# A rewritten order table for an attention and mixing kernel: GpSimd work set apart from VectorE work with two SBUF inputs

## The chip, the core and the metric

The kernel runs on one core of a Trainium2 chip. A core has five instruction queues that run side by side and wait for each other by semaphores: TensorE (PE, with its weight loads shown as PEld), VectorE (DVE), ScalarE (ACT), GpSimd (POOL) and SyncE (SP), which here issues every DMA. The metric is the device time of one execution in microseconds.

## The reference

Four batches of 768 tokens with 8 heads of 64 go through a windowed attention and then a mixing block.

```python
k_sum = k.reshape(B, H, nb, 32, D).max(axis=3)          # 24 block maxima
v_sum = v.reshape(B, H, nb, 32, D).mean(axis=3)         # 24 block means
scores_l = scale * q @ k.T     # only |i - j| < 16 is kept
scores_s = scale * q @ k_sum.T + log(32)
a = exp(scores - max); a = a / (sum(a) + 1e-9)
x = a @ concat(v, v_sum)                                # then [B, 768, 512]
theta = x @ w_theta
y = w_tok_r @ (x * cos(theta)) + w_tok_i @ (x * sin(theta))
u = x + y
out = u + max(u @ w_ch, 0)
```

The four weight matrices come as 64-bit floats and are turned into 32-bit floats on the core.

## The kernel before

The program is first written down as a list of 2525 operations with their dependences (`Program.op`), and then issued in the order of a table, `ORDER` (`Program.issue`). A row of the table such as `V+743,-707` names an engine (P, A, V, G, S for PE, ACT, DVE, POOL, SP) and the numbers of operations, each as a step from the number before. So the table sets two things: in which order each engine meets its instructions, and on which engine an operation runs where several may run it. Buffers of the pools `r` (52 of 512 words), `w` (17 of 1024), `l` (19 of 384) and the 8 PSUM banks `b` are handed out in the order of the table. No engine is told to wait for another but by data and by buffers.

```python
def hi_op(dst, src, n, reads, writes, psum=False):
    op(f"AV {'psum' if psum else 'cast'} {n}", lambda e: copy(e, dst(), src()), reads, writes)
def lo_op(dst, src, hi, n, reads, writes):
    op(f"VG tt {n}", lambda e: V[e].tensor_tensor(dst(), src(), hi().bitcast(F32), op=ALU.subtract), reads, writes)
...
    for row in order.split():
        e, seqs = names[row[0]], row[1:].split(",")
...
    o.fn(e)
```

The letters at the start of an operation's kind are the engines that may run it: "AV cast" runs on ACT or DVE, "VG tt" (two tensors in SBUF) on DVE or POOL, "GAV part" and "GAV join" on any of the three.

The work, by the lines of the profile:

- Weights: each of 32 slices is loaded and turned from 64-bit to 32-bit by a magnitude (L2288 on ACT, L2290 on DVE), a clamp (L2292, DVE or POOL), a shift (L2293, DVE) and two joins of bits with two inputs (L2295, L2297, DVE). Later slices are split into a rounded high part (L2244, "AV cast") and the rest (L2250, "VG tt") for matmuls at full rate.
- Attention, 24 tiles of 128 tokens (six a batch): scores (L2390, PE), a masked minimum from PSUM (L2416, DVE), exponentials (L2420, ACT), a turn of the probabilities (on PE for the first six tiles; later by a copy into 16-bit halves, a transposing DMA and a copy back, L2244 "part" and "join"), the product with v (L2432, PE), division by the sum (L2436 to L2445). For batches 1 to 3 the keys are gathered into `k` (L2244, POOL or ACT).
- Mixing: theta (L2489, L2485, PE), its reduction, sine and cosine (L2495 to L2510, ACT, DVE or POOL), two products with x (L2517, DVE or POOL), their split (L2244, L2250), and the mixing matmuls: L2534 for batch 0, L2554 for batches 1 to 3. The result is added to u (L2568, DVE).
- Channels: w_ch is combined for Strassen's seven products (L2592, DVE or POOL), then for each batch u is combined (L2617, DVE or POOL), split (L2244 to ACT or DVE, L2250 to DVE or POOL, into the pool `l`), multiplied (L2628, PE), kept (L2244 from PSUM) and finished (L2642, L2644, DVE).

Of the kernel before, what the change touches and what calls it, by code (L numbers as in the profile page):

```python
# [19 lines left out]
B, H, S, D = 4, 8, 768, 64  # L20
# [35 lines left out]
S-646,-16,-6,-44,+48,+53,-41,-14,+8  # L56
V-3
S+1,+13,+42,-51,-55
V+48
A+53  # L60
S-44
V+45
S+28,-69
V-17
S-43
V+102,-57
P-14,+1,+1,+1,+1,+1,+1
V+66
S+8
P-73,+32  # L70
V+34
S+177
V-175
P-55
V+56
S-40,+50
P-64
V+20,+13
A-9
V+11,-16  # L80
S+259
V-257,+11
P-30
A+21
V-5
A+21
V+16
A-30
P-39
A+50  # L90
P-32
A+33
S+33
V+7
A-55
V+34
P-50
S+223
V-151
S+154  # L100
V-153
P-53
V+8
P-26
A+19
S+297
V-265
A-21
V+42
A-71  # L110
G+51
P-20
S+54
P+141
A-220
V-3
A+29
S+329
V-140
G+3  # L120
V-176
P-29
V+222,+1,-15
P-194
S+374
A-161
V-194
A-32
V+224,-223
A+13  # L130
S+589
P-351
A-250
V+13,+21,+187,-207
A+209
V-15
A+18
V-20
P-23
S-132  # L140
A+174
V+40,-58
A+5
P-256
G+79
V+1
A+148
P+43
S+370
V-560  # L150
P-80
A+254
P-25
A+42
V-197
S+218
A-209
P+147
V-155
A+178  # L160
S-81
G-88
A+168
V-171
A+231
P-81
V+576,-513,+1,+14
S-18
P-35
A+43  # L170
V-3,+1
A+1
P-66
V+79
A-54
S-157
V-7,+217
P-38
S+837
A-876  # L180
V-148
S+553
P-380
A+57
V-81
A+67
V-215
P+253
A-66,+40,+1
V-40,-39  # L190
A+40
V-180
P+221
A-80
V+23,+1
P+171
V-170
A+39
V+341
A-324  # L200
V-210,+1
P+277
V-45,+15,+2
G-261
V+245,-254
S+541
A-391
V+106
P-41,-26
A+27  # L210
S+35
P-20
V-80
G+1
V-130
A+168
P+27
V+50,-12
A-23
S+307,-289  # L220
V+19
P+126
A-177
S-145,+223
V-63,+428,-442,+15
P-42
V-182
S+551
V-3,-259
A-39  # L230
S+37
V-283
P+179
A+78
G+300
V-351
A+52,-15
G+341
V-283
P-80  # L240
A+39
P-80
V+108
G-287
S+22
V+505
A-223,-233,+150
V-149
P+108
A+78  # L250
S+272
A-287
V+43
A-42
P+16
V+25
A-104
V-185
S+536
P-309  # L260
A+68
V+7
G-116
A+107
V+236
G+164
S-679
A+280
P-44
A+42,-27,-14  # L270
S+281
A-226
V-119
S+351
V-350
A+1
G+370,-1
P-330,+159
V-82
G+252  # L280
P-328
V+312
P-275
V-265
P+251
V+51
A-36
P+29
S+35,-275
V+134,+1  # L290
P+39
V+23,+1
S+290
V-289
P+135
A-83
S+307
V-280
A-25
V-41,+67  # L300
A-104,-168
P+322
V-116
A+28
V-270
G+205
V+116
# [2454 lines left out]
```

## Time and profile before

| | us |
|---|---|
| median of 3 runs (range) | 509.34 (506.67 to 513.09) |
| the profiled execution | 505.22 |
| its span, first to last instruction | 503.4 |
| PE busy | 449.0 |
| DVE busy | 418.7 |
| ACT busy | 261.3 |
| POOL busy | 233.9 |

Busy is the time in which at least one instruction of the engine ran; about 2 us of the profiled execution lie outside the span. An instruction's duration in the profile runs from its start to its end, and it may start while the one before it on the engine still ends, so durations add up to some more than the busy time. In what follows the span is cut into five stretches, at the last mixing matmul of each batch: 0 to 184.5 us (batch 0), 184.5 to 281 (batch 1), 281 to 367.8 (batch 2), 367.8 to 432 (batch 3) and the rest, 432 to 503.4, which is channel work alone.

### The profile page before, as it was taken

What the parts mean: (1) busy time and instruction counts of PE and PEld (TensorE: products, weight loads), DVE (VectorE), ACT (ScalarE), POOL (GpSimd) and SP (SyncE); (2) the same over time, 40 slices, a digit from 0 to 9 for tenths busy, and PEclk for the clock granted to TensorE, in tenths of its full rate; (3) what the DMA queues carried; (4) which work ended last, traced back from release to release, by engine and by line L of the source; (5) the groups of instructions that cost most, each with busy time, mean ns of one, the idle gap of its engine ahead of it and who ended that gap; (6) DMA issues with size and microseconds to landing.
All of it is one profiled execution on the core that took longest, in us unless ns stands there. A gap on an engine that the chain in (4) does not pass through costs nothing.

```text
span 503.4 us, 10037 instructions
## 1 busy us (share of the span) xinstructions
PE 449.0 (89%) x3520; PEld 347.7 (69%) x3520; DVE 418.7 (83%) x1063; ACT 261.3 (52%) x572; POOL 233.9 (46%) x262
## 2 busy tenths in 40 slices
PE   8898988898979598898999799989999959977886
PEld 6474544444656466776887688878888848977875
DVE  3889999998997979987789888775558683899997
ACT  1498995866645546674866475814423301423230
POOL 0113476353675766453352644351432572645661
PEclk9999999999998889998999989999999988999899
DMA  8999978798976649537577656669463402431045
GB/s 293 348 306 280 311 210 211 190 223 247 177 218 140 179 107 204 137 103 225 143 199 167 171 114 145 143 156 250 144 203 114 175 12 80 157 125 64 16 167 210
DMA packets 108578, 88.88 MB, mean 177 GB/s; under 512 B 61936, under 2 KB 88304, under 8 KB 108528
## 3 DMA queue, kind: packets, MB, share of 16 engines
q1 hardware_dynamic: 108528, 88.24, 63.7%
q8 instruction: 28, 0.46, 0.4%
q14 instruction: 22, 0.18, 0.1%
HBM read 55.19 MB, written 18.87 MB: 147 GB/s over the span
## 4 chain that ended last, share of the span: by engine, by line
PE 21%; DVE 21%; issue 6%; POOL 6%; DMA 5%; ACT 3%; SPq 1%; DVEq 0%; POOLq 0%; ACTq 0%
PE b L2554 11%; PE b L2628 7%; DVE r L2244 4%; POOL r L2250 3%; DVE l L2250 3%; DVE r L2250 2%; DMA r<-r 2%; PE b L2485 2%; DVE r L2416 2%; ACT r L2420 2%; DVE r L2644 1%; POOL r L2244 1%; DMA u_scratch<-r 1%; POOL r L2517 1%; DMA w<-wch 1%
## 5 line engine op out<-in xcount | busy, mean ns | idle before, releaser
L2554 PE MATMUL b<-w,r 128*128 128x512 f32 x432 | 158.6, 406 | 11.0 <-DVE r L2250 7.5
L2554 PE MATMUL b<-r,r 128*128 128x256 f32 x432 | 122.6, 284 | 0.5 <-DVE st L2416 0.4
L2554 PEld LDWEIGHTS b<-w,r 128*128 128x128 f32 x432 | 82.5, 191 | 34.1 <-DVE r L2250 8.5
L2420 ACT ACTIVATE r<-r,st 128x118 f32<-128x118 f32 x192 | 63.9, 387 | 44.8 <-DVE st L2416 44.3
L2554 PEld LDWEIGHTS b<-r,r 128*128 128x128 f32 x432 | 83.1, 192 | 2.2 <-DVE st L2416 0.7
L2244 POOL COPY r<-r 128x1024 uint16<-128x1024 uint16 (+2 forms) x43 | 53.3, 1249 | 51.6 <-ACT r L2420 20.7
L2485 PE MATMUL b<-w,r 128*128 128x512 f32 x216 | 56.7, 400 | 1.0 <-DVE r L2250 0.9
L2534 PE MATMUL b<-w,r 128*128 128x512 f32 x96 | 47.3, 623 | 4.4 <-DVE w L2297 3.9
L2416 DVE CUSTOM_DVE_ANT_0 r<-b,cs 128x118 f32<-128x118 f32 x192 | 45.2, 271 | 5.8 <-PE b L2390 4.9
L2485 PEld LDWEIGHTS b<-w,r 128*128 128x128 f32 x216 | 38.5, 188 | 10.5 <-DVE r L2250 1.3
L2244 DVE COPY r<-r 118x1024 uint16<-118x1024 uint16 (+2 forms) x40 | 36.6, 923 | 8.3 <-ACT r L2420 4.2
L2250 POOL TENSOR_TENSOR l<-r,l 128x384 fp32r<-128x384 f32 x26 | 31.1, 1205 | 21.1 <-PE b L2628 13.3
L2628 PE MATMUL b<-l,r 128*128 128x384 f32 x192 | 37.9, 342 | 3.3 <-DVE r L2642 2.4
L2628 PEld LDWEIGHTS b<-l,r 128*128 128x128 f32 x192 | 34.1, 191 | 4.8 <-DVE r L2642 3.5
L2292 POOL TENSOR_SCALAR r<-r 128x512 f32<-128x512 f32 (+1 forms) x21 | 14.6, 701 | 48.4 <-DVE r L2290 30.5
L2628 PE MATMUL b<-l,w 128*128 128x384 f32 x144 | 30.6, 346 | 6.0 <-DVE r L2244 4.0
L2432 PEld LDWEIGHTS b<-v,r 118*64 118x64 f32 x768 | 25.5, 140 | 14.3 <-issue 5.1
L2244 POOL COPY k<-kn 128x188 f32<-128x188 f32 x47 | 22.9, 503 | 26.9 <-PE b L2390 24.0
L2244 ACT CAST l<-r 128x384 fp32r<-128x384 f32 x38 | 18.4, 513 | 32.5 <-PE b L2628 23.0
L2244 ACT COPY r<-r 128x944 uint16<-128x944 uint16 (+2 forms) x25 | 29.1, 1168 | 11.2 <-DMA r<-r 5.7
L2534 PEld LDWEIGHTS b<-w,r 128*128 128x128 f32 x96 | 17.8, 195 | 24.2 <-issue 16.0
L2432 PE MATMUL b<-v,r 118*64 118x65 f32 x768 | 29.1, 228 | 5.3 <-POOL r L2244 1.5
(98 smaller groups left out, 900.0 us busy)
## 6 DMA issues: line engine op xcount, KB each, us to landing
u_scratch<-r SPq DMA_DIRECT2D x40, 256.0 KB, 3.4
v<-vg SPq DMA_DIRECT2D x48, 195.0 KB, 3.4
r<-qg SPq DMA_DIRECT2D x24, 256.0 KB, 4.9
r<-u_scratch SPq DMA_DIRECT2D x32, 192.0 KB, 3.1
out<-r SPq DMA_DIRECT2D x32, 192.0 KB, 2.0
kn<-kT SPq DMA_DIRECT2D x6, 798.0 KB, 6.9
r<-u_scratch SPq DMA_DIRECT2D x16, 256.0 KB, 3.3
w<-wti SPq DMA_DIRECT2D x6, 512.0 KB, 6.6
```

The source lines that it names most:

```text
L2244: (nc.scalar.copy if e == "ACT" else V[e].tensor_copy)(dst, src)
L2250: op(f"VG tt {n}", lambda e: V[e].tensor_tensor(dst(), src(), hi().bitcast(F32), op=ALU.subtract), reads, writes)
L2292: op(f"VG ts {n}", lambda e: V[e].tensor_scalar(f(), f(), MOST, LEAST, ALU.min, ALU.max), [], [f_ref])
L2416: op("V ttr", lambda eng, n=n: nc.vector.tensor_tensor_reduce(e.get()[:, n], sc[n % 2].get()[:, 2 * a + n // 2], mask(m), -SCALE, 3.0e38, ...
L2420: op("A exp", lambda eng, n=n: nc.scalar.activation(e.get()[:, n], e.get()[:, n], AF.Exp, bias=st.get()[:, n:n + 1], scale=-1.0), [(st, n) ...
L2432: mm("av", [lambda n=n, g=g: nc.tensor.matmul(xa.get()[ROW[g], n], t.get()[:, n, ROW[g]], v[g].get()[:NK, NH * a + n], start=True, stop=Tr ...
L2485: calls = [lambda t=t, xx=xx, k=k, c=c, wt=wt: nc.tensor.matmul(th.get(), xx.get()[:, c], wt.get()[:, k], start=(c == 0 and t == 0), stop= ...
L2517: op(f"VG tt {DM}", lambda e, z=z, hc=hc: V[e].tensor_tensor(z(), xn[b, i].get().rearrange("p h d -> p (h d)")[:, None, hc].broadcast_to(( ...
L2534: nc.tensor.matmul(acc, zb[b, c // 2, s].get()[:, r, c % 2 * P:(c % 2 + 1) * P], wt[r, th].get()[:, 0], start=(clear and s == r == 0), sto ...
L2554: nc.tensor.matmul((ma[c].get(), half(2, c)())[th], z[k].get()[:, r, c * P:(c + 1) * P], wt[r, th].get()[:, kw], start=(s == r == t == 0 a ...
L2628: calls = [lambda t=t, p=p, x=x, k=k: nc.tensor.matmul(acc.get(), a(p, k, m), x.get(), start=(first and k == 0 and t == 0), stop=(k == 1 a ...
L2644: op(f"V {'ttp' if extra is None else 'tt'} {HT}", lambda e: nc.vector.scalar_tensor_tensor(y.get(), x.get(), 0.0, y.get(), ALU.max, ALU.a ...
```

## The change

Only the table `ORDER` is new; the 2525 operations, their dependences, the pools and their sizes are the same. The lines of the file move up by 75 (L2250 becomes L2175, L2244 L2169, L2617 L2542, L2420 L2345).

```diff
 ORDER = """
-G+3
-P+1,+1,+1,+1,+1,+1,+1,+1,+1,+1,+1,+1,+1,+1,+1,+1,+1,+1,+1,+1,+1,+1,+1,+1,+1,+1,+1,+1,+1
-V+743,-707,+3,+215,+3,+663,-59,-181
+V+71,-3,+221,+486
+S-715,-8,+67
+V+1,+1,+1,+1,+1
...
```

413 operations change their engine. POOL gives up 150 and takes 93, so it runs 201 instead of 258. DVE runs 898 instead of 871, ACT 509 instead of 479, PE 563 and SP 354 as before. By kind:

| operation | POOL | DVE | ACT |
|---|---|---|---|
| two inputs, 384 wide (L2250, L2617) | 45 to 18 | 43 to 70 | |
| two inputs, 512 wide (L2250, L2517) | 41 to 33 | 83 to 91 | |
| two inputs, 256 wide (L2250, L2592) | 12 to 11 | 10 to 11 | |
| turn, part and join (L2244) | 43 to 26 | 40 to 45 | 25 to 37 |
| keys into k (L2244) | 47 to 36 | | 25 to 36 |
| v's block means (L2244) | 7 to 4 | 6 to 2 | 3 to 10 |
| magnitude of the weights, 512 wide (L2288, L2290) | | 14 to 5 | 6 to 15 |

Two places of the new order. The first is the end of POOL's queue, in the channel work: `l<-r,l` is the rest of a split (L2250, now L2175), `r<-r,r` a combination of u (L2617, now L2542). Before, its last twelve instructions:

```order
L2617 TENSOR_TENSOR r_5460<-r_5001,r_5201 128x384
L2250 TENSOR_TENSOR l_5485<-r_5355,l_5470 128x384
L2250 TENSOR_TENSOR l_5501<-r_4786,l_5283 128x384
L2250 TENSOR_TENSOR l_5511<-r_5235,l_5435 128x384
L2250 TENSOR_TENSOR l_5567<-r_5001,l_5543 128x384
L2250 TENSOR_TENSOR l_5586<-r_5410,l_5572 128x384
L2250 TENSOR_TENSOR l_5597<-r_4563,l_5521 128x384
L2250 TENSOR_TENSOR l_5616<-r_5400,l_5529 128x384
L2617 TENSOR_TENSOR r_5628<-r_5218,r_5368 128x384
L2250 TENSOR_TENSOR l_5647<-r_5285,l_5642 128x384
L2250 TENSOR_TENSOR l_5672<-r_5449,l_5670 128x384
L2250 TENSOR_TENSOR l_5674<-r_5628,l_5638 128x384
```

And now:

```order
L2175 TENSOR_TENSOR l_5150<-r_4801,l_5100 128x384
L2175 TENSOR_TENSOR l_5286<-r_4930,l_5121 128x384
L2542 TENSOR_TENSOR r_5323<-r_5143,r_5053 128x384
L2175 TENSOR_TENSOR l_5364<-r_5053,l_5102 128x384
L2175 TENSOR_TENSOR l_5433<-r_4518,l_5407 128x384
L2175 TENSOR_TENSOR l_5458<-r_5244,l_5362 128x384
L2175 TENSOR_TENSOR l_5536<-r_4982,l_5534 128x384
L2175 TENSOR_TENSOR l_5569<-r_5262,l_5564 128x384
L2175 TENSOR_TENSOR l_5604<-r_5405,l_5594 128x384
L2175 TENSOR_TENSOR l_5664<-r_5517,l_5581 128x384
L2542 TENSOR_TENSOR r_5666<-r_4611,r_5221 128x384
L2175 TENSOR_TENSOR l_5670<-r_5666,l_5668 128x384
```

The kinds are the same, but the numbers at the names, which count up through the program, are spread wider: the twelve results reached from l_5485 to l_5674 before, and now from l_5150 to l_5670. What lies between went to DVE. Behind the last mixing matmul of batch 3, POOL had 32 instructions of these two kinds and now has 13.

The second place is ACT's queue around the exponentials of attention tile 9, in the first stretch. `r<-r,st` of L2420 (now L2345) are exponentials, four a half tile; `128x8x118` is a part, `118x2x512` a join. Before:

```order
L2420 ACTIVATE r_1375<-r_1375,st 128x118
L2420 ACTIVATE r_1387<-r_1387,st 128x118 x2
L2420 ACTIVATE r_1282<-r_1282,st 128x118 x2
L2420 ACTIVATE r_1375<-r_1375,st 128x118
L2420 ACTIVATE r_1387<-r_1387,st 128x118
L2495 ACTIVATE w<-b_1246 128x512
L2420 ACTIVATE r_1375<-r_1375,st 128x118 x2
L2244 COPY r_1019<-r_1375 128x8x118
L2420 ACTIVATE r_1387<-r_1387,st 128x118
```

And now:

```order
L2169 COPY r_1430<-r_1423 128x8x118
L2345 ACTIVATE r_1412<-r_1412,st 128x118 x2
L2169 COPY r_588<-r_1412 128x8x118
L2420 ACTIVATE w<-b_1277 128x512
L2169 COPY r_1535<-r_1432 128x1024
L2169 COPY r_1540<-r_1514 118x2x512
L2169 COPY r_1566<-r_1533 118x2x512
L2345 ACTIVATE r_1517<-r_1517,st 128x118 x4
L2169 COPY r_843<-r_1517 128x8x118
```

Tile 9's two joins and one of its two parts, which DVE and POOL ran before, now stand in ACT's queue, the joins ahead of the next tile's exponentials (`r_1517`); the L2420 of these rows is the line of the theta step, L2495 before.

## Rows read from the trace of the kernel before

**Rows 1.** The page: busy time by engine, and the chain that ended last

```profile
PE 449.0 (89%) x3520; PEld 347.7 (69%) x3520; DVE 418.7 (83%) x1063; ACT 261.3 (52%) x572; POOL 233.9 (46%) x262
...
PE 21%; DVE 21%; issue 6%; POOL 6%; DMA 5%; ACT 3%; SPq 1%; DVEq 0%; POOLq 0%; ACTq 0%
```

**Rows 2.** Busy by stretch: PE, PEld, DVE, ACT, POOL, clock, DMA share, GB/s

```profile
0.00:184.50 184.50, 161.69 (x1532) 100.87 (x1532) 161.81 (x512) 119.28 (x286) 85.14 (x117) 0.96 0.84 232
184.50:281.00 96.50, 89.33 (x690) 73.14 (x690) 84.47 (x209) 61.49 (x119) 47.15 (x54) 0.98 0.68 169
281.00:367.80 86.80, 82.43 (x681) 68.99 (x680) 63.34 (x171) 43.72 (x93) 35.69 (x37) 0.98 0.64 160
367.80:432.00 64.20, 58.16 (x318) 50.50 (x317) 41.74 (x66) 16.29 (x31) 27.83 (x25) 0.95 0.37 120
432.00:503.40 71.40, 57.41 (x309) 54.23 (x308) 67.28 (x109) 20.48 (x44) 38.10 (x32) 0.98 0.33 116
```

**Rows 3.** Timeline of 474 to 480 us: start, us, what, count

```profile
474.38 1.36 DVE L2250 TENSOR_TENSOR l<-r,l 128x384 fp32r<-128x384 f32 x1
...
475.28 3.90 POOL L2250 TENSOR_TENSOR l<-r,l 128x384 fp32r<-128x384 f32 x3
...
475.66 1.37 DVE L2644 SCALAR_TENSOR_TENSOR r<-r,r 128x384 f32<-128x384 f32 x1
...
476.96 0.55 DVE L2642 TENSOR_TENSOR r<-b,r 128x384 f32<-128x384 f32 x1
```

**Rows 4.** DVE instructions of single lines: duration ns min/median/max, first and last start us

```profile
L2416 DVE CUSTOM_DVE_ANT_0 r<-b,cs x192: 230/270/289, 15.9 to 330.4; 128x118 f32<-128x118 f32 x192
...
L2644 DVE SCALAR_TENSOR_TENSOR r<-r,r x24: 544/560/1369, 423.7 to 497.5; 128x384 f32<-128x384 f32 x24
L2644 DVE SCALAR_TENSOR_TENSOR r<-b,r x8: 543/548/552, 444.9 to 499.4; 128x384 f32<-128x384 f32 x8
...
L2250 DVE TENSOR_TENSOR l<-r,l x30: 543/548/1377, 370.6 to 485.1; 128x384 fp32r<-128x384 f32 x30
L2250 DVE TENSOR_TENSOR r<-w,r x13: 671/686/792, 190.2 to 413.1; 128x512 fp32r<-128x512 f32 x13
...
L2244 DVE COPY r<-r x40: 635/752/1814, 73.7 to 351.4; 118x1024 uint16<-118x1024 uint16 x17, 128x1024 uint16<-128x1024 uint16 x12, 128x944 uint16<-128x944 uint16 x11
...
L2244 DVE CAST r<-r x30: 278/419/1620, 124.0 to 427.1; 128x512 fp32r<-128x512 f32 x22, 128x256 fp32r<-128x256 f32 x8
```

**Rows 5.** Groups by line and shape: count, busy us, mean ns, idle before

```profile
L2250 POOL TENSOR_TENSOR l<-r,l 128x384 fp32r<-128x384 f32 x26 | 31.1, 1205 | 21.1 <-PE b L2628 13.3 <-ACT l L2244 5.1 <-DVE l L2244 2.6
L2250 DVE TENSOR_TENSOR r<-r,r 128x512 fp32r<-128x512 f32 x28 | 29.9, 1074 | 0.4
...
L2250 DVE TENSOR_TENSOR l<-r,l 128x384 fp32r<-128x384 f32 x30 | 23.8, 809 | 0.2 <-PE b L2628 0.2
...
L2644 DVE SCALAR_TENSOR_TENSOR r<-r,r 128x384 f32<-128x384 f32 x24 | 19.2, 820 | 0.4
...
L2244 DVE COPY r<-r 118x1024 uint16<-118x1024 uint16 x17 | 18.3, 1088 | 3.0 <-DMA r<-r 2.0 <-POOL r L2292 1.1
...
L2244 DVE CAST r<-r 128x512 fp32r<-128x512 f32 x22 | 16.6, 755 | 2.5 <-POOL r L2517 1.2 <-POOL r L2244 1.0
...
L2244 ACT COPY r<-r 118x1024 uint16<-118x1024 uint16 x7 | 9.5, 1355 | 6.0 <-DMA r<-r 4.4 <-DVE r L2250 1.6
```

**Rows 6.** The chain in order of time: start us, us, a run of channel matmuls

```profile
488.27 10.28 PE b L2628 x57
```

**Rows 7.** Who waited for whom: us in total, times, longest us

```profile
ACT r L2420 <- DVE st L2416: 44.3, 25, 5.9
...
POOL l L2250 <- PE b L2628: 13.3, 6, 4.2
...
PEld b L2534 <- DVE r L2297: 7.5, 3, 5.8
```

More of the change, by code (lines that the diff above doesn't have):

```diff
@@ new lines @@
+P-71
+V+181,-102
+G+172
+S-61
+P-155
+G+37
+S+270
+V-262
+S+8
+P+165
+V-202,-12
+S+73
+A-57
+V-2,-3
+A+7
+V-5,-16
+A+7
+P-42
+V+36
+A+19
+V+212
+P-266
+S+248
+A-196
+V-16
+P-35
+V+266
+A-228
+P-37
+V+267
+A-229
+P+16
+S+36
+A-54
+V+215
+P-250
+V+249,-189
+A-6
+P-15
+V+212,-175
+S+166
+P-187
+G+189
+A-204
+V+28
+A+187
+S+174
+P-388
+V+28
+A+184,+1
+G-193
+P+233
+S+89
+V-327
+A+212
+V-3,-13
+A+17
+V-227,+1
+S+52
+V-38
+A-13
+V+14
+P+282
+V-278
+A+194
+V-193
+A+204
+S+368
+A-551
+V-20
+P+163
+A+43
@@ new lines @@
+G-185
+P+172
+V+53
+A-82
+V+81
+P-38
+V+41
+S-20
+V+5
+A-189
+V-38
+P+160
+A+71
+S-8
+V-184,+1,+1
+A+202
+P-82
+V+80,-15,-1
+A+19,-42,-14
+P-26
+S-17
+A-125
+P+143
+A-47
+V-74
+S+533
+V-559
+S+547
+P-360
+A-39
+V+64,-121
+P+82
+G-72
+A+128
+V-41
+A+28
+V-27
+G-40
+V+41
+P+156
+A-133,+1
+G-209
+S+247
+A-22
+V+27
+S+306
+V-413
+A+24
+G+426,+181
+V-775
+P+225
+A-80
+V+24
+S-160
+V+161
+A+56
+V+37
+P-52,-302
+V+303
+P-27,+109
+V-299,+191
+A-40
+V+103
+P-36
+S+322
+V-270,-264
+P+226
+S-128
+A-95
+G+143
@@ new lines @@
+V+67
+S-181
+V+219
+P-64
+V+76
+A-36
+V-13
+S+322
+V-321
+S+31
+V+297
+P-355
+G-41
+S+145
+V-64,+37
+A-13
+S+296
+V+5
+P-364
+A+80
+V-40
+A+39
+V+309
+A-311
+V+43
+S-18
+P-101
+V+59
+A+6
+V-260
+A+272,-13
+V+41
+P-65
+V+66
+A-105
+V-190
+P+391
+A-139
+G-61
+V+105
+A-66
+V+77
+P-38
+S+413
+V-598
+A-76
+V+184
+P+40
+V+253
+A-185
+G-291
+V+284
+P-60
+V+76,-116
+A+77,-76
+P+61,-21,+1
+A+78,-1
+V+222
+P-145
+V-133
+A+41
+S+252
+P-292
+A+1
+V+52
+G+253
+S-26
+V-1
+P-265
+A+27
+V-39,+1
+A+54
+P+78
+S-343
@@ new lines @@
+V+445
+P-391
+V+373,-426
+P+54
+A+376
+V-429
+P+482
+V-201
+P-207
+V+425,-59
+A-439
+V+482
+G+24
+V-6,-382
+P-65
+V-52
+P+74
+V+426,-499
+A+502
+V-20
+G+6
+A-366
+V-121,+422
+A+18
+V-439
+A+440
+P-390
+A+392
+V+39,-385
+A+329
+P-208
+A+265
+V-205
+A+164
+P-223
+A+208
+G+18
+A-393
+P+168
+V-167
+S+393
+P-225
+V-167
+P+20
+V+24
+P-23
+A-20
+S-386
+V+827
+S-449
+P+52
+S+315
+A-358
+P+20
+V+46,+358,-60
+P-342
+V-21
+P+43
+G+10
+P-9,+4,+2,+4
+S+25
+V-77
+S+35
+P-17
+G+370
+S-53
+A+108,-16,-62
+P-344
@@ new lines @@
+S+49
+V-48
+P-286
+V-153
+P-16
+S+555
+V-437
+S+535
+V-252
+P-399
+V+400
+P-385
+V+386
+A+166
+P-563
+V+557,+7
+P-551
+A+572
+P-583
+V+17,-3
+S+4
+P-14
+V+331
+S+309,-248
+P-390
+S+331
+V-1
+P-326,+2
+A+484
+P-99
+S+46
+V-423
+S+530
+P-388
+S-192,+573
+P-380
+S+580
+P-579
+S+479
+P-245
+A-233
+P+55
+V-54,+393
+P-338
+V-54
+G+393
+P-161
+A-231
+V+383
+P-329
+A-53
+V+492
+P-323
+V+237,-405
+P+53
+S+278
+V-329
+S-151
+P+318
+G-168
+P+109
+V-107
+P+227
+V+176
+A-352
+P+57
+G+216
+V-525
+P+438
+G-185
@@ new lines @@
+V-91
+A-211
+P+111
+A-110
+V+164,-45
+P-42
+A+91
+V-14
+P-43
+V+78
+G-188
+P+78
+S+121
+V-31
+A-166
+P+111
+V-110,+186,-188
+P+113
+V+123
+A-183
+P+62
+V+74
+G-135
+V+1
+P+64
+V+44
+A-107
+P+58
+V+76
+A-133
+V+149
+P-132
+V-16,+106
+A-104,+62
+V+111,-18
+A+2
+V-26,+46
+P+30,+1
+V-49,+192,-350
+A+168
+V-58
+P-95
+A+193
+V-101,-45
+P-5
+G+54
+V-3,+1
+G+5
+S-86
+V+87
+P-56
+V+90
+P-86
+V+180
+P-183
+A+72
+P-114
+A+100
+V-5
+A+7
+V-3
+P+61,+1
+A+1
+V-182,+175
+A-106
+P-47
+V+113,+24
+P-135
+V+133,-34
```

3593 lines of the change are left out of this document (1548 added, 2045 removed).

## The prediction

> **What bounds the kernel now.** I read the page first, then busy time by stretch, then the durations of single lines, the timeline, and the waits. On the page PE is busy 449.0 of 503.4 us and DVE 418.7, and the chain that ended last spends 21% of the span on each [rows 1]. One bound for the whole program does not come out of that, so the stretches decide [rows 2]. In the first stretch (184.5 us) DVE is busy 161.8 and PE 161.7, and most of what both leave idle is the start. In the last (71.4 us) DVE is busy 67.3, 94%, and PE 57.4: DVE bounds it. In the three between, PE is busy 229.9 of 247.5 us and DVE 189.6: PE bounds them, with gaps that others make.
>
> Part of DVE's busy time is no work. A masked minimum from PSUM (L2416) takes 230 to 289 ns in all 192 cases, and L2644 with one input in PSUM 543 to 552 in all eight. The same L2644 with both inputs in SBUF goes from 544 to 1369, L2250 from 543 to 1377, casts and copies from SBUF to SBUF from 278 to 1620 and from 635 to 1814 [rows 4]. The timeline shows when: at 475.66 us an L2644 takes 1.37 us while POOL runs three subtractions from 475.28 to 479.18, and the L2642 behind it, with one input in PSUM, takes 0.55 beside the same POOL work; at 474.38 an L2250 takes 1.36 [rows 3]. So a VectorE instruction with two SBUF inputs waits while GpSimd reads SBUF, and so does a one-input copy.
>
> How much is lost: count times (mean less the duration alone). For two inputs, 28 x (1074 - 686) + 30 x (809 - 545) + 24 x (820 - 545) ns = 10.9 + 7.9 + 6.6 = 25.4 us for the three costliest forms [rows 4, 5]; the ten other such forms, worked the same way, bring it to about 47. For one input, 22 x (755 - 419) + 17 x (1088 - 752) = 7.4 + 5.7 = 13.1 for the two costliest, about 34 with the eleven others. Of DVE's 419 us some 81 are waiting. By stretch (two inputs + one input): 18 + 11 in the first, 7 + 12, 4 + 3 and 5 + 4 in the middle, 15 + 3 in the last.
>
> **The change, part by part.**
>
> *GpSimd does less.* Priced alone, its instructions in the five stretches come to 69, 43, 28, 24 and 34 us before and 59, 36, 14, 13 and 13 in the new order (196 to 135). The largest part is 27 of 45 subtractions 384 wide, at 1205 ns on POOL [rows 5].
>
> *VectorE does more.* The 27 subtractions cost 27 x 0.545 = 14.7 us there; nine more two-input instructions at 0.41 to 0.69 add 6; nine magnitudes, four block means, five absolute values and some clamps fewer, against five turns and five normalisations more, take back about 5. Net: some +15 us. By stretch +1, 0, -5, +22 and -3: channel work is drawn forward, ahead of batch 3's last mixing matmul.
>
> *ScalarE does more.* Twelve turns, eleven gathers of keys, seven block means and nine magnitudes more, less five normalisations: about +21 us on an engine busy 261 of 503 [rows 1]. In the first stretch it goes from 119 busy to about 130 of 184 [rows 2]: I cost it at nothing there, because ACT's longest wait is for DVE's minima, 44.3 us in 25 waits, most of them in that stretch [rows 7]. If that cover is gone, a join at 1355 ns [rows 5] stands ahead of exponentials and delays a tile by itself; that is a rival below.
>
> *Less waiting.* The overlap is not forbidden by any wait, only planned away, so the loss lies between nothing and what chance gives. By chance the two-input loss would be 47 x 135/196 = 32, times 260/224 instructions = 38; if the plan held to the instant, 0. I take 15, nearer the plan, because an instruction that meets the other is held and the order then falls back into step. One-input copies are not spared: 34 x 135/196 = 23. Bounds for DVE's total loss are thus 23 and 61, against 81; I take 38.
>
> A place where a rule speaks against this change: the rows above show one-input casts at 419 ns alone and up to 1620 [rows 4], so planning around two inputs alone treats 47 of 81 us. The Trainium skill, "SBUF — State Buffer", section "Who interferes with whom", says the same: a GpSimd instruction also excludes VectorE's copies, casts and tensor-scalar operations in their two-port modes, whoever starts first holding the ports for its whole instruction. By a rule of two inputs alone the 23 us left to one-input copies would go too, and the sum below would come out some 10 us lower; by the page's rule they stay. The trace agrees with the page.
>
> *First stretch.* DVE now: 161.8 busy, 29 of it waiting. New: +1 of work, loss 5 + 10 = 15, so 148 busy, 14 less. PE has some 2 us less ahead of the cut (three steps of theta and scores move behind it). Of DVE's 14 I count 12, since the start and the weights' DMA (share 0.84 [rows 2]) do not shrink. 184.5 becomes 172.5.
>
> *Middle.* The new order puts 25 channel products of three matmuls ahead of the last mixing matmul, where nine stood: 48 matmuls at 10.28/57 = 0.18 us [rows 6], 8.6 us, and the 2 from the first stretch: PE's work grows by 10.6. DVE's work grows by 17 and its loss falls from 35 to 18, so it stays as busy as it was. PE's gaps, 247.5 - 229.9 = 17.6 us, shrink with the loss; I take 4 off. 247.5 becomes 254.
>
> *Last stretch.* PE has 48 matmuls fewer: 309 x 0.18 = 55.6 becomes 47. DVE: 67.3 - 18 = 49 of work, less 3, plus a loss of at most half a subtraction (0.5 us) for each of the 13 left on POOL, 6.5: 52.5. With the 4 us that it is idle now, 56 to 57 instead of 71.4, 15 less.
>
> Sum: 505.2 (the profiled execution: span 503.4 and 2 around it) - 12 + 6.5 - 15 = 484.7. The median of the three runs, 509.34, lies 0.8% above the profiled execution; I put half of that on top and say 486.
>
> **The rivals.**
>
> *Overlap by chance (493).* The table sets orders, no times. If the engines drift by more than an instruction, a GpSimd instruction meets two-input work as often as before: the loss is 61 instead of 38. For it: of the two-input instructions in the rows, more than half met POOL, and waits of 6 to 13 us [rows 7] shift the plan. Against it: POOL has a third less to run. First stretch -6, middle +7, last -13: 505 - 12 = 493.
>
> *VectorE's time was hidden anyway (501).* The chain gives DVE 21% and PE 21% [rows 1]; if the first stretch is held by DMA and by the start, and the 22 us of channel work drawn forward cost PE gaps in the fourth stretch (DVE 41.7 busy of 64.2 becomes about 63), then 0, +10 and -14: 501. For it: the DMA share of 0.84. Against it: waits for DMA are small beside DVE's in the rows.
>
> *ScalarE's queue (525, slower).* One mechanism: part and join copies now stand on ACT ahead of exponentials, as the order shows at tile 9. A join waits for its transposing DMA, and everything behind it waits as well: the next half tile's exponentials, the turn, the product with v. The first stretch has 22 more one-input copies on ACT (39 to 61). If each holds the queue by 1.36 us of work and half as much of waiting, that is 22 x 2 = 44 us of ACT; ACT has 184.5 - 119.3 = 65 us idle, so it decides from the point where two thirds of that idle time cannot be used. Price: 30 us exposed over the first two stretches, less 10 of the gains: 505 + 20 = 525.
>
> *PE becomes the bound everywhere (466).* If the waits of the matmuls on DVE (L2534 on L2297, 7.5 us [rows 7]) and on POOL's subtractions go, and the granted clock, 0.95 to 0.98 of 2.4 GHz [rows 2], stays full because PE no longer pauses: first -18, middle -1, last -20: 466.
>
> That the change doesn't do what it says is the first rival.
>
> **How the numbers follow.** Forecast 0.38; overlap by chance 0.20; hidden 0.20; ScalarE 0.13; PE 0.09. The range 466 to 514 holds all but ScalarE, the far side of hidden and half of PE, so some 0.81. A measurement of this kernel can tell about 2%: its own runs span 506.67 to 513.09. Faster by over 2% means under 499: the forecast but for 0.03 of it, PE, three quarters of chance, and little of hidden: 0.35 + 0.09 + 0.15 + 0.02 = 0.61. Slower by over 2% (over 519.5): ScalarE, 0.13. The rest, 0.26, is within 2%.
>
> **What would show it.** Right: DVE's L2250 forms fall to a mean near 600 (384 wide) and 750 ns (512 wide), while casts keep maxima over 1000; POOL busy falls to 150 to 170 us, DVE to 380 to 400; the last stretch is under 60 us and starts before 430. Wrong in the first step: L2250's mean stays over 800. Wrong in the last: DVE no longer over 90% busy there and the stretch still 65 or more. ScalarE is at fault if ACT's busy share in the first 180 us passes 80% or if its L2345 waits grow over 60 us. If PE's idle time in the middle grows beyond 25 us, drawing channel work forward was the cost.

## The result, and the profile after

The changed kernel takes 464.65 us (median of four runs, 461.76 to 468.18) against 510.5 us for the kernel before in the same comparison: a ratio of 0.911, 95% interval 0.902 to 0.920. The direction was forecast and the size was not: 486 was said, with a low end of 466, so the time lies just below the range and the gain is about twice the forecast. Of the executions below, one (640.8 us, in the first experiment) ran at a granted clock of 0.63 and is left out of its median.

The profiled execution took 464.35 us. Its page, busy time by engine and the chain that ended last (against [rows 1]):

```profile
PE 433.7 (94%) x3520; PEld 340.6 (74%) x3520; DVE 391.0 (85%) x1090; ACT 282.9 (61%) x589; POOL 159.1 (34%) x205
...
PE 37%; DVE 30%; ACT 7%; DMA 6%; issue 5%; POOL 1%; SPq 1%; DVEq 0%; ACTq 0%; POOLq 0%
```

PE runs the same 3520 matmuls in 15.3 us less and now fills 94% of the span; its idle time falls from 54.4 to 28.9 us. Together that is the 40.8 us by which the span is shorter. The same five stretches, cut as before (against [rows 2]; columns us, PE, PEld, DVE, ACT, POOL, clock, DMA share, GB/s):

```profile
0.00:169.10 169.10, 154.59 (x1549) 98.31 (x1550) 148.31 (x499) 128.15 (x280) 71.05 (x111) 0.99 0.90 252
169.10:259.10 90.00, 86.37 (x764) 71.57 (x763) 79.23 (x255) 72.93 (x153) 40.74 (x54) 1.00 0.84 197
259.10:329.90 70.80, 69.56 (x532) 58.90 (x532) 48.03 (x121) 37.00 (x69) 13.66 (x15) 1.00 0.66 157
329.90:409.90 80.00, 76.63 (x420) 67.20 (x419) 66.37 (x123) 24.31 (x45) 17.39 (x15) 1.00 0.40 125
409.90:462.60 52.70, 46.51 (x261) 44.66 (x260) 49.07 (x96) 20.50 (x46) 16.28 (x12) 1.00 0.41 143
```

The first stretch is 15.4 us shorter, the three in the middle 240.8 instead of 247.5, the last 52.7 instead of 71.4. The clock column, 0.95 to 0.98 in every row before, is 0.99 to 1.00.

VectorE's two-input instructions, by shape (count, busy us, mean ns, idle before; against [rows 5]):

```profile
L2175 DVE TENSOR_TENSOR r<-r,r 128x512 fp32r<-128x512 f32 x32 | 23.8, 748 | 2.4 <-DMA u_scratch<-r 1.2 <-DMA r<-r 0.9
L2175 DVE TENSOR_TENSOR l<-r,l 128x384 fp32r<-128x384 f32 x40 | 23.1, 604 | 0.1
...
L2169 DVE COPY r<-r 118x1024 uint16<-118x1024 uint16 x17 | 15.2, 898 | 6.9 <-DMA r<-r 6.8
L2569 DVE SCALAR_TENSOR_TENSOR r<-r,r 128x384 f32<-128x384 f32 x24 | 13.6, 590 | 0.1
...
L2169 DVE CAST r<-r 128x512 fp32r<-128x512 f32 x20 | 11.2, 565 | 0.7 <-POOL r L2169 0.7
```

The three two-input forms fall from means of 1074, 809 and 820 ns to 748, 604 and 590; their durations alone are 681 and 545. Their tails are not gone, nor are those of the one-input casts (single lines: ns min/median/max, first and last start; against [rows 4]):

```profile
L2175 DVE TENSOR_TENSOR l<-r,l x40: 539/545/1409, 323.2 to 449.4; 128x384 fp32r<-128x384 f32 x40
...
L2169 DVE CAST r<-r x27: 281/418/2135, 133.4 to 361.7; 128x512 fp32r<-128x512 f32 x20, 128x256 fp32r<-128x256 f32 x7
```

Counted as in the prediction (count times mean less the duration alone, over all forms), some 40.7 us of DVE's time is waiting, 16.6 with two inputs and 24.1 with one; before it was 81. Such sums move by a us or two with the duration that is taken as alone. Who waited for whom (against [rows 7]):

```profile
POOL l L2175 <- PE b L2553: 40.6, 8, 12.1
...
ACT r L2345 <- DVE st L2341: 14.1, 16, 3.7
```

The exponentials wait 14.1 us for the minima instead of 44.3. POOL waits longer: its subtractions stand 40.6 us behind channel matmuls, where before it was 13.3. POOL can afford it, since it has 1% of the chain that ended last, where it had 6.

### The profile page after: what moved, and what is told of

Same layout as the page of the kernel before. It is cut to its first block, busy times and chain, and to the rows that moved or that the text cites. A ratio compares the mean times of both kernels' runs of the same rounds, so it can differ in the third digit from the quotient of the medians.

```text
span 462.6 us, 9964 instructions
## 1 busy us (share of the span) xinstructions
PE 433.7 (94%) x3520; PEld 340.6 (74%) x3520; DVE 391.0 (85%) x1090; ACT 282.9 (61%) x589; POOL 159.1 (34%) x205
## 4 chain that ended last, share of the span: by engine, by line
PE 37%; DVE 30%; ACT 7%; DMA 6%; issue 5%; POOL 1%; SPq 1%; DVEq 0%; ACTq 0%; POOLq 0%
PE b L2479 23%; PE b L2553 8%; PE b L2410 5%; DVE r L2341 3%; DMA r<-r 3%; DVE r L2169 3%; DVE r L2175 2%; DVE r L2220 2%; DVE l L2175 2%; DVE r L2370 2%; ACT r L2169 2%; DVE r L2567 1%; DMA r<-u_scratch 1%; ACT r L2345 1%; DVE vt L2267 1%
## 5 line engine op out<-in xcount | busy, mean ns | idle before, releaser
L2479 PE MATMUL b<-w,r 128*128 128x512 f32 x432 | 153.9, 397 | 3.3 <-DVE r L2493 3.3
L2479 PE MATMUL b<-r,r 128*128 128x256 f32 x432 | 120.9, 280 | 1.1 <-DVE r L2493 1.1
L2479 PEld LDWEIGHTS b<-w,r 128*128 128x128 f32 x432 | 81.0, 188 | 22.9 <-DVE r L2493 3.6
L2479 PEld LDWEIGHTS b<-r,r 128*128 128x128 f32 x432 | 81.4, 188 | 2.8 <-DVE r L2493 1.8
L2345 ACT ACTIVATE r<-r,st 128x118 f32<-128x118 f32 x192 | 63.1, 385 | 16.2 <-DVE st L2341 14.1
L2410 PE MATMUL b<-w,r 128*128 128x512 f32 x216 | 57.1, 401 | 1.6 <-DVE r L2175 0.8
L2169 ACT COPY r<-r 128x944 uint16<-128x944 uint16 (+2 forms) x37 | 42.9, 1172 | 8.2 <-DMA r<-r 7.4
L2459 PE MATMUL b<-w,r 128*128 128x512 f32 x96 | 45.5, 602 | 2.5 <-DVE r L2370 1.3
L2410 PEld LDWEIGHTS b<-w,r 128*128 128x128 f32 x216 | 38.4, 188 | 11.8 <-DVE r L2175 1.3
L2175 POOL TENSOR_TENSOR l<-r,l 128x384 fp32r<-128x384 f32 x16 | 20.9, 1309 | 75.0 <-PE b L2553 40.6
L2169 POOL COPY r<-r 128x1024 uint16<-128x1024 uint16 (+2 forms) x26 | 33.9, 1304 | 36.0 <-ACT r L2345 16.9
L2169 DVE COPY r<-r 118x1024 uint16<-118x1024 uint16 (+2 forms) x45 | 36.0, 809 | 10.0 <-DMA r<-r 8.5
L2169 ACT CAST l<-r 128x384 fp32r<-128x384 f32 x39 | 19.3, 515 | 37.6 <-DVE r L2542 14.8
L2357 PEld LDWEIGHTS b<-v,r 118*64 118x64 f32 x768 | 25.0, 137 | 13.3 <-issue 5.9
L2357 PE MATMUL b<-v,r 118*64 118x65 f32 x768 | 28.9, 225 | 4.4 <-DVE st L2341 2.1
L2459 PEld LDWEIGHTS b<-w,r 128*128 128x128 f32 x96 | 17.3, 190 | 19.8 <-issue 16.9
L2420 ACT ACTIVATE w<-b 128x512 f32<-128x512 f32 x24 | 14.2, 594 | 23.3 <-DVE r L2442 5.7
L2553 PE MATMUL b<-l,w 128*128 128x384 f32 x144 | 27.7, 336 | 0.1
L2175 DVE TENSOR_TENSOR r<-r,r 128x512 fp32r<-128x512 f32 (+1 forms) x36 | 25.3, 711 | 2.4 <-DMA u_scratch<-r 1.2
```

The costliest lines, as they stand in the source:

```text
L2169: (nc.scalar.copy if e == "ACT" else V[e].tensor_copy)(dst, src)
L2345: op("A exp", lambda eng, n=n: nc.scalar.activation(e.get()[:, n], e.get()[:, n], AF.Exp, bias=st.get()[:, n:n + 1], scale=-1.0), [(st, n) ...
L2357: mm("av", [lambda n=n, g=g: nc.tensor.matmul(xa.get()[ROW[g], n], t.get()[:, n, ROW[g]], v[g].get()[:NK, NH * a + n], start=True, stop=Tr ...
L2410: calls = [lambda t=t, xx=xx, k=k, c=c, wt=wt: nc.tensor.matmul(th.get(), xx.get()[:, c], wt.get()[:, k], start=(c == 0 and t == 0), stop= ...
L2420: op(f"A psumb {DM}", lambda e: nc.scalar.activation(r(), th.get(), AF.Identity, bias=MAGIC, scale=1.0 / TWO_PI), [th], [R])
L2459: nc.tensor.matmul(acc, zb[b, c // 2, s].get()[:, r, c % 2 * P:(c % 2 + 1) * P], wt[r, th].get()[:, 0], start=(clear and s == r == 0), sto ...
```

## The experiments

Each run was timed beside the kernel before on the same chip. Stretches of the experiments are cut at the same matmuls.

**Sequence or engines?** First the new sequence with the 413 changed engine choices put back (the numbers of the table stay in the new order, the letters are the old ones).

```diff
 for each step of the new ORDER:
-  engine = the new one
+  engine = the one it had in the old ORDER
```

> The new sequence of operations, but each operation on the engine that it had before (GpSimd 258 operations again). If the gain comes from the engine choices (less work on GpSimd), 490 to 510 us and GpSimd busy over 215; if it comes from the sequence itself, 465 to 480. The lock theory (VectorE held up by GpSimd's reads): VectorE's waiting on two-input work is back at 35 us or more, and the time between 485 and 505.

Measured: 531.03 us (three executions), ratio 1.045 (1.036 to 1.054), slower: outside every time that was expected, the 485 to 505 of the lock theory (VectorE held up by GpSimd's reads) included. No trace of it is read here.

Then the converse, the old sequence with the new engine choices.

```diff
 for each step of the old ORDER:
-  engine = the old one
+  engine = the one it has in the new ORDER
```

> The old sequence with the new engine choices (GpSimd 201 operations). If the engine choices alone make the gain, 465 to 480 us; if the sequence does, 500 to 520. The lock theory: two-input waiting falls from 47 to about 30 us by the smaller load of GpSimd alone, time 485 to 500.

Measured: 515.66 us, ratio 1.015 (1.006 to 1.024). The page of this run:

```profile
PE 450.7 (88%) x3520; PEld 351.2 (69%) x3520; DVE 398.9 (78%) x1090; ACT 280.5 (55%) x587; POOL 162.9 (32%) x205
```

POOL does as little as in the changed kernel, and DVE's waiting, counted as above, is 45 us, nearly as low as the changed kernel's 41. Yet PE is idle 61.1 of 511.8 us, more than before, and the time is longer than the 485 to 500 that the lock theory gave: the first stretch is 4 us shorter than before (180.4), the three in the middle together 14 us longer (261.4). So neither half of the table gains alone, and less waiting on DVE is not enough by itself: the sequence must fit the engines. Which waits make the halves slower was not followed up.

**What is the waiting worth?** In the kernel before, 224 of the 236 two-input VectorE instructions with both inputs in SBUF (all but the twelve absolute values of L2505) become reductions over single elements, which read one input of the same size; subtractions, products and bit joins on VectorE are left out with that, and so are 24 of the last sums of the channel work (L2644). Order, engines and GpSimd's instructions stay.

```diff
+def one(dst, src):
+    nc.vector.tensor_reduce(dst, src[..., None], op=ALU.max, axis=AX.X)
...
-    lambda e: V[e].tensor_tensor(dst(), src(), hi().bitcast(F32), op=ALU.subtract)
+    lambda e: one(dst(), src()) if e == "DVE" else V[e].tensor_tensor(...)
```

> The kernel before, with every VectorE instruction that has two SBUF inputs replaced by a one-input reduction over single elements (a copy at one element a cycle); this leaves out the subtractions, products and bit joins of VectorE. Order and engines as before. The lock theory: these instructions no longer stretch (maximum under 0.8 us where they reached 1.78), 47 us of VectorE waiting are gone, the granted clock rises to 0.99 and the time is 465 to 485. If the order or the balance of the engines is the cause, it stays at 495 to 510.

Measured: 463.79 us, ratio 0.915 (0.907 to 0.922): as fast as the changed kernel, with the old sequence and the old engines. By shape, two of the reductions, two one-input copies and POOL's subtraction 384 wide:

```profile
L2244 DVE TENSOR_REDUCE r<-r 128x512 fp32r<-128x512 f32 x28 | 18.6, 672 | 0.4 <-DMA r<-r 0.4
L2247 DVE COPY r<-r 118x1024 uint16<-118x1024 uint16 x17 | 17.6, 1044 | 3.3 <-DMA r<-r 1.9 <-issue 1.3
L2244 DVE TENSOR_REDUCE l<-r 128x384 fp32r<-128x384 f32 x30 | 15.7, 540 | 0.8 <-PE b L2632 0.7
L2247 DVE CAST r<-r 128x512 fp32r<-128x512 f32 x22 | 15.7, 713 | 6.1 <-POOL v L2371 2.8 <-DMA u_scratch<-r 2.0 <-POOL r L2519 1.1
L2254 POOL TENSOR_TENSOR l<-r,l 128x384 fp32r<-128x384 f32 x26 | 26.2, 1018 | 18.0 <-PE b L2632 13.3 <-ACT l L2247 3.5 <-DVE l L2247 0.8
```

The reductions take 672 and 540 ns, the two-input forms' time alone, with the same GpSimd instructions beside them; the copies stay stretched (1044 and 713 against 752 and 419 alone). So 47 us of DVE's two-input waiting are gone and the time is 45 us shorter. It is not DVE's waiting alone that went: the hold-up is mutual. POOL's 26 subtractions fall from a mean of 1205 ns [rows 5] to 1018, all of POOL from 233.9 us busy to 208.0, and no run parts what POOL's 26 us were worth from what DVE's 47 were. The stretches say where the time went:

```profile
0.00:168.30 168.30, 156.38 (x1532) 99.60 (x1536) 143.26 (x512) 118.81 (x284) 75.20 (x117) 0.99 0.95 252
168.30:261.30 93.00, 88.29 (x689) 73.23 (x689) 76.68 (x210) 63.01 (x122) 44.71 (x55) 0.98 0.71 180
261.30:348.90 87.60, 83.90 (x682) 70.43 (x680) 59.50 (x170) 43.00 (x92) 32.78 (x36) 0.96 0.64 156
348.90:408.60 59.70, 56.54 (x318) 49.09 (x317) 36.78 (x66) 16.15 (x31) 24.14 (x25) 1.00 0.39 130
408.60:466.30 57.70, 54.00 (x308) 53.23 (x307) 51.49 (x109) 20.43 (x44) 31.22 (x32) 1.00 0.40 142
```

First 16 us shorter, the middle 7, the last 14. The changed kernel has -15, -7 and -19, but there 48 matmuls, 8.6 us, have moved from the last stretch into the middle; for equal matmuls its middle gains more than this run's, and its last stretch less.

A reduction also drops the wait for the second input's data. So the run was made again with the helper of low halves reading the later of its two inputs, the cast.

```diff
-    lambda e: one(dst(), src()) if e == "DVE" else ...
+    lambda e: one(dst(), hi().bitcast(F32)) if e == "DVE" else ...
```

> The kernel before with one-element reductions in the place of all 224 two-input VectorE instructions, as in the run that gave 464 us, but the 85 of the helper for low halves now read the later input, the cast that the subtraction waits for, so that no wait for data is dropped with the second input (the subtractions, products and bit joins are left out). Theory: the gain of 45 us is VectorE's waiting for SBUF alone, and the time stays 464 within 5. Rival: part of it was the dropped wait for the cast; the time is 470 or more.

Measured: 465.41 us, ratio 0.916 (0.910 to 0.921). The dropped wait for the cast was worth nothing that can be measured. In both runs the bit joins, products and last sums already read the input that is made last; 17 combinations (13 of L2617, 4 of L2592) still read the first alone.

The same replacement in the changed kernel, with the same left out:

> The same replacement in the changed kernel, where 17 us of two-input waiting are left. The lock theory: 455 to 464 us, a gain of at most 10, and within 20 us of the kernel before with the same replacement. If the new order is better for another reason, it keeps a lead of 30 us or more over the kernel before with the same replacement.

Measured: 453.30 us, ratio 0.891 (0.882 to 0.899). That is 11 us below the changed kernel, for the 16.6 us of two-input waiting that the new table still leaves, and 2 us below the range expected. It also says what two-input waiting does not account for: with that waiting gone from both, the new table is still 10.5 us faster than the old (453.3 against 463.8). So some 35 us of the change's 45 go with two-input waiting and some 10 with something else. DVE's waiting with one input is some 16 us in this run and 32 in the other, counted the same way, but no run takes that away alone.

**Stretch by stretch.** Is the middle shorter by its own waiting, or by a better start? The reductions go into the middle alone (92 instructions, whose subtractions, products and bit joins are left out), then into both ends alone (132).

```diff
+turn = [0]
+def pick():
+    turn[0] += 1
+    return 76 < turn[0] <= 168
...
-    one(dst(), src()) if e == "DVE" else ...
+    one(dst(), src()) if e == "DVE" and pick() else ...
```

> The kernel before, with the one-element reductions of the run on both ends and middle put only in the place of the 92 two-input VectorE instructions from 184.5 to 432 us (the subtractions, products and bit joins that these would do are left out). Theory: waiting of VectorE in the middle counts there by itself, through TensorE's gaps; the middle shrinks from 247.5 us by 6 to 8, the first 184.5 and the last 71.4 us stay within 2, and the time is about 503. Rival: the middle only profits from what the first stretch does better (clock and head start); then the middle stays within 2 us of 247.5 and the time is 508 to 510.

Measured: 496.77 us, ratio 0.978 (0.973 to 0.984). Stretches (first, middle in two pieces, last):

```profile
0.00:185.70 185.70, 163.47 (x1535) 102.01 (x1538) 162.56 (x512) 119.31 (x286) 85.64 (x117) 0.95 0.86 230
185.70:363.80 178.10, 169.64 (x1370) 141.22 (x1367) 135.59 (x379) 105.22 (x211) 77.17 (x90) 0.99 0.68 169
363.80:421.60 57.80, 56.38 (x318) 49.09 (x317) 36.76 (x66) 16.15 (x31) 24.21 (x25) 1.00 0.41 136
421.60:494.30 72.70, 59.41 (x308) 57.13 (x306) 65.82 (x109) 20.26 (x44) 36.44 (x32) 0.93 0.32 113
```

> The complement: the reductions only in the place of the 76 two-input VectorE instructions ahead of 184.5 us and the 56 behind 432 us of the kernel before, whose subtractions, products and bit joins are left out. Theory: the gains add up by stretch; the first is 16 us shorter, the last 13, the middle stays within 2 us of 247.5, and the time is about 480. Rival: the head start and the warmer clock carry over; the middle is 5 us or more shorter as well, and the time is 472 or less.

Measured: 477.37 us, ratio 0.942 (0.935 to 0.950). The same stretches:

```profile
0.00:167.30 167.30, 155.98 (x1536) 99.55 (x1540) 143.56 (x512) 118.97 (x285) 74.91 (x117) 0.99 0.94 254
167.30:351.90 184.60, 172.69 (x1369) 143.07 (x1366) 148.36 (x379) 105.92 (x213) 83.69 (x90) 0.97 0.66 164
351.90:417.20 65.30, 58.62 (x318) 50.58 (x318) 41.45 (x66) 16.16 (x31) 27.37 (x25) 0.95 0.37 119
417.20:474.90 57.70, 53.65 (x308) 53.19 (x306) 51.30 (x109) 20.41 (x44) 32.08 (x32) 1.00 0.40 142
```

The gains are local and add up. In the first run the middle is 235.9 us instead of 247.5 (more than the 6 to 8 us expected) and the ends are within 1.3; in the second the ends are 17.2 and 13.7 us shorter and the middle is 249.9. 10.5 and 29.9 us by the medians, 40 of the 45 of both together. In the middle some 15 us of two-input waiting were worth 11.6 in this execution: 7.7 from PE's gaps (17.6 to 9.9), 3.9 from its busy time (229.9 to 226.0, with the clock nearer 1.00). The two runs with reductions everywhere give 7.2 (above) and 10.1 us (reading the later input) for the same middle, so the worth is half to three quarters of the waiting.

**Reading or mere presence?** Behind each of the changed kernel's GpSimd steps comes a filler: in one run a copy that reads a scratch tile, in the other a memset that only writes it.

```diff
+pr.nc, pr.scratch = nc, wpool.tile([P, 352], F32, tag="zz", name="zz")
+nc.gpsimd.memset(pr.scratch, 0.0)
...
 o.fn(e)
+if e == "POOL":
+    self.nc.gpsimd.tensor_copy(za, za)    # the other run: memset(za, 0.0)
```

> The changed kernel with one GpSimd copy of a 128x352 float32 scratch tile onto itself behind each GpSimd step, some 200 of them; results unchanged. Theory (GpSimd instructions that read SBUF hold up VectorE's two-input instructions and two-port copies): some 90 us more of such reading raise VectorE's loss from 41 us to 65 or more, the mean of the 384-wide subtraction goes from 604 to over 700 ns, and the time is 480 to 495. Rival (it is the order of the products, or GpSimd's own load, that decides): same time as with the writing filler, within 1%.

> The changed kernel with one GpSimd memset of the same 128x352 float32 scratch tile behind each GpSimd step; results unchanged. Theory: a memset reads nothing, so VectorE's loss stays near 41 us, the 384-wide subtraction's mean near 604 ns, and only GpSimd's own lateness costs something: 465 to 475 us, at least 10 us less than with the reading filler. Rival: same time as with the reading filler, within 1%; or, if writing holds the ports as well, VectorE's loss rises with this filler too.

Measured: 488.51 us with the reading filler (ratio to the kernel before 0.961, 0.954 to 0.968), 476.41 with the writing one (0.938, 0.933 to 0.943), a little over the 465 to 475 expected. DVE's waiting becomes 66.5 and 51.1 us instead of 40.7; the mean of the 384-wide subtraction, 604 ns, becomes 644 and 586, not the 700 expected of the reading filler. The times alone don't separate the theories, since the fillers are not of one size, as the groups by shape show for the reading and then the writing one:

```profile
L2142 POOL COPY zz<-zz 128x352 f32<-128x352 f32 x201 | 129.9, 646 | 1.0
```

```profile
L2142 POOL MEMSET zz<- 128x352 f32 x201 | 84.4, 420 | 0.9
```

Single meetings do. With the reading filler (timeline: start us, us, what), a subtraction that takes 0.545 alone takes 0.82 beside it:

```profile
426.10 0.81 POOL L2142 COPY zz<-zz 128x352 f32<-128x352 f32 x1
426.49 0.82 DVE L2180 TENSOR_TENSOR l<-r,l 128x384 fp32r<-128x384 f32 x1
```

With the writing one, both instructions run as if alone:

```profile
463.47 0.39 POOL L2142 MEMSET zz<- 128x352 f32 x1
463.50 0.54 DVE L2180 TENSOR_TENSOR l<-r,l 128x384 fp32r<-128x384 f32 x1
```

Over all two-input instructions that overlap a filler and no other GpSimd instruction in the trace, the time beyond the duration of their form alone is 216 ns on average for the 17 that met the copy and nothing (-1 ns) for the 8 that met the memset. So it is GpSimd's reading that holds them. One-input copies, casts and tensor-scalar operations differ: 220 ns for 15 beside the copy, but also 150 ns for 9 beside the memset. The expectation that a memset leaves DVE's waiting near 41 us failed; those are part of the reason, and that fillers push GpSimd's own reads off the places that the table planned may be the rest, which is not shown. The Trainium skill, "SBUF — State Buffer", "Who interferes with whom", says that a two-input VectorE instruction contends with a GpSimd instruction that reads and not with one that only writes, and that a VectorE instruction in a two-port mode, such as a copy or a cast, contends with GpSimd, with no such exception; these rows agree, on few instructions.

**Which choices carry it?** The new sequence with only the 49 changed subtractions 384 wide back on their old engines (38 from VectorE to GpSimd, 11 the other way), and the converse, only these on their new ones.

```diff
 for each step of the new ORDER:
-  engine = the new one
+  engine = the old one if its kind is "VG tt 384" (the other run: if it is not)
```

> The changed kernel with its new sequence, but the 49 subtractions 384 wide that changed engine (38 from GpSimd to VectorE, 11 the other way) put back on their old engines. Theory (gains are made stretch by stretch, by less GpSimd reading beside VectorE): these run from some 330 us on, so the first three stretches stay within 3 us of 169, 90 and 71, and the fourth and last give back 12 to 25 us together; the time is 477 to 490. Rival (sequence and choices only work as one plan, wherever they are broken): over 500, with the early stretches changed too.

Measured: 471.82 us, ratio 0.927 (0.924 to 0.931). The fourth and last stretch:

```profile
331.60:411.50 79.90, 76.99 (x420) 67.29 (x419) 66.90 (x108) 24.54 (x46) 34.43 (x29) 1.00 0.41 125
411.50:469.70 58.20, 48.76 (x260) 46.05 (x258) 49.48 (x84) 20.64 (x46) 29.95 (x24) 0.95 0.37 129
```

The early stretches stay, as the theory of local gains has it, but only 7 us are given back, 5.5 of them in the last stretch, less than the 12 expected: POOL is twice as busy there (30 for 16 us), and DVE's waiting grows by some 12 us in all.

> The complement: the new sequence with all 364 other changed engine choices put back, only the 49 subtractions 384 wide on their new engines. Theory: the last two stretches keep 12 to 25 us of the gain, so the time lies that much below the 532 of the new sequence with all old engines: 507 to 520; the first three stretches are together over 360 us, against 330 in the changed kernel. Rival: the subtractions carry the gain; under 490.

Measured: 529.15 us, ratio 1.038 (1.032 to 1.043), so 2 us under the run with all old engines, which is within the spread of both, and not the 12 or more expected. Its first stretch:

```profile
0.00:203.40 203.40, 165.91 (x1550) 103.68 (x1551) 159.54 (x514) 119.76 (x285) 79.77 (x117) 0.95 0.75 213
```

203.4 us instead of 169.1, with DVE busy 78% of it. VectorE's waiting explains little of that: it is 57 us in all here, 16 more than in the changed kernel and 24 less than in the kernel before, while the time is 64 us longer than the one and 20 longer than the other. The engines wait for each other; which wait does it was not followed up. The new sequence belongs to its engine choices, above all those of the attention stretches; the subtractions that I priced first were the smaller part.

**A version that beats both?** The changed kernel with GpSimd's 17 copies 1024 wide on ScalarE.

```diff
 for each step of the new ORDER:
+  engine = ACT if it is POOL and the kind is "GAV join 1024" or "GAV part 1024"
```

> The changed kernel with the 17 copies 1024 wide that GpSimd still does (24.6 us of it) on ScalarE instead. If what is left of VectorE's loss (41 us) still costs time, and ScalarE's queue has room (it is idle 180 of 463 us): loss 36 or less, time 457 to 463. Rival (ScalarE's queue: a join holds up the exponentials behind it): slower than 465, up to 475, and the first two stretches longer than 169 and 90.

Measured: 469.65 us, ratio 0.923 (0.920 to 0.926), 5 us slower than the changed kernel, which was timed in another comparison (the intervals of the two ratios, 0.920 to 0.926 and 0.902 to 0.920, just touch). The page:

```profile
PE 438.3 (94%) x3520; PEld 342.5 (73%) x3520; DVE 383.0 (82%) x1090; ACT 300.8 (64%) x606; POOL 133.5 (29%) x188
```

DVE's waiting did fall, to 32 us, and the time rose: the rival came true in its time and in its place (first and second stretch 172.3 and 91.5 instead of 169.1 and 90.0), though ScalarE's queue as the cause is only argued. Of the 5.5 us by which its span is longer, PE's busy time has 4.6, at a lower clock. No run that computes the whole beats the changed kernel.

## Why the prediction was wrong in size

**Right: what waits, and how much.** GpSimd's reading and VectorE's two inputs [rows 3, 4] are the main cause: the five runs with reductions take that meeting away, on both engines, and some 35 of the 45 us go with it; what makes the other 10 is open. The waiting left was forecast as 15 + 23 us and measured as 16.6 + 24.1, but the 15 was picked between 0 and 38 with no working that gives it, so that it came this near is partly luck. Elsewhere POOL's busy time was forecast as 150 to 170 and measured as 159, DVE's as 380 to 400 and measured as 391; L2250's means as near 600 and 750, measured 604 and 748; the casts kept maxima over 1000. DVE in the first stretch is 148.3 busy for a forecast 148, PE in the last 46.5 for 47.

**Wrong: the middle, by 13.2 us of the 20 that the sum was off.** The step that failed was "PE's gaps, 247.5 - 229.9 = 17.6 us, shrink with the loss; I take 4 off. 247.5 becomes 254." Measured: 240.8. Three terms:

- PE's work, forecast +10.6. Before, the lost shares of the clock [rows 2] are 0.02 x 96.5 + 0.02 x 86.8 + 0.05 x 64.2 = 6.9 us. That is an upper estimate, since PE was busy in 11.2 of the 13.6 us at half clock there; half of 11.2 is 5.6. So at full clock PE's 229.9 us are some 223 to 224. Now it is 232.6 at 1.00: +8 to +10. This term was about right.
- The clock, forecast nothing in the middle: -6 to -7. The rows had it, and I used them only in a rival.
- The gaps, forecast -4: 17.6 becomes 8.2, so -9.4.

Why I took 4: I read "PE bounds the middle" as "DVE's waiting there hardly counts". But much of PE's gaps came of that waiting: the run with reductions in the middle alone takes 7.7 of the 17.6 us of gaps away, and the runs return half to three quarters of the 15 us of two-input waiting, where I had counted a quarter of the loss that goes. A stretch of the kernel before shows how the clock goes with it (columns as in [rows 2]):

```profile
398.70:405.20 6.50, 6.50 (x40) 5.80 (x39) 5.28 (x6) 0.72 (x2) 6.50 (x6) 1.00 0.01 3
405.20:411.70 6.50, 3.23 (x19) 2.58 (x18) 6.43 (x10) 0.48 (x1) 4.40 (x5) 1.00 0.00 0
411.70:418.50 6.80, 4.62 (x13) 3.63 (x14) 2.46 (x4) 0.51 (x1) 4.34 (x5) 0.50 0.12 39
418.50:425.00 6.50, 6.50 (x38) 5.79 (x38) 2.74 (x5) 0.62 (x1) 1.01 (x1) 1.00 0.25 76
```

PE runs without a gap, then is busy 3.2 of 6.5 us while DVE is busy 6.4 of them; then the granted clock is 0.50, that is 1.2 GHz, for 6.8 us, and full again after it. The same timeline has a bit join at 1.78 us and one at 1.11 in front of that gap, 0.69 alone, and a cast at 1.13, 0.42 alone: some 2.2 us of waiting ahead of a gap of 5.4. The kernel before has six such spells inside its span, 30.6 us together, each begun in or just behind a gap of PE of 1.1 to 5.4 us; ahead of four of them DVE was busy for 6.4 to 6.5 of 6.5 us. The changed kernel has one, of 3.4 us. Not every gap brings one: PE pauses 3.3 us from 341.3 us on in the changed kernel, at full clock. Where a waiting DVE instruction makes such a gap, it can so be paid for twice, as the gap and as slower matmuls behind it.

**First and last: -15.4 for -12, -18.7 for -15.** In the first I counted 12 of DVE's 14, for a start and weights that would not shrink; DVE's 13.5 came through in full, and the clock's lost share falls from 0.04 to 0.01, some 5 us of matmul time. That most of what both engines leave idle there is the start was misread: the first 25 us hold 10.2 of DVE's 22.7 idle us and 3.2 of PE's 22.8.

```profile
0.00:25.00 25.00, 21.76 (x238) 14.04 (x241) 14.81 (x54) 7.23 (x17) 2.78 (x7) 1.00 0.95 321
```

In the last, DVE is busy 49 where I had 52.5, and idle 3.6 for my 4.

**The rivals.** "PE becomes the bound everywhere (466)" is nearest to what came, in time and in the full clock: -18, -1 and -20 against -15.4, -6.7 and -18.7. It is not all of it: in the last stretch DVE, busy 49.1 of 52.7 us, still bounds, and PE is busy 46.5. It got 0.09, because full clock and vanished gaps looked like two wishes; here they went together, since each half-clock spell came with a gap. "Overlap by chance", at 61 us of waiting, is refuted by the 40.7 that are left. "VectorE's time was hidden anyway" is refuted by the run that takes away 47 us of VectorE's waiting, with POOL's 26, and gains 45. "ScalarE's queue" did not decide here: ACT is busy 76% of the first stretch and its exponentials wait less than before. Some danger there is: the run with 17 more copies on ScalarE lost 5 us, though its cause is not shown.

## What to carry to other kernels

Where VectorE instructions with two SBUF inputs have durations that spread upward beside GpSimd work, price that waiting from count and mean less the duration alone. In this kernel most of it was on the path, also in stretches that PE bounds, where PE had gaps and a granted clock below 1.00 and both came back together; whether it is so elsewhere has to be measured. To learn what it is worth before planning an order, replace these instructions by one-input ones of the same length and look at the time, and remember that GpSimd's own waiting goes with it. An order and its engine choices are one plan; test them together.

## What was not expected

- GpSimd's memsets do not hold two-input VectorE instructions (-1 ns on average, 8 of them), but the one-input instructions that met one took 150 ns longer (9 of them).
- Taking away 47 us of waiting on an engine that is busy 83% of the span, and 26 us of POOL's with it, was worth 45 us of time in a kernel whose PE was busy 89%.
- The old sequence with the new engine choices had DVE's waiting down to 45 us and was still 1.5% slower than the kernel before (0.6 to 2.4).
